# Identity products in the planned TensorE gaps of the first batch, written to a corner of a PSUM bank

## The chip, the cores and the metric

The kernel runs on one core of a Trainium2 chip. The time is the device time of one execution, in microseconds. Before the change eight executions took 437.73 to 443.24 us, with a median of 440.87 us.

## The reference

The reference is a cosine attention followed by a feed-forward layer with a quick-GELU gate:

```python
q_n = q / (np.linalg.norm(q, axis=-1, keepdims=True) + 1e-06)
k_n = k / (np.linalg.norm(k, axis=-1, keepdims=True) + 1e-06)
scores = np.matmul(q_n, k_n.transpose(0, 1, 3, 2)) / tau
attn = softmax(scores); out = np.matmul(attn, v)     # 8 batches, 12 heads, 448 tokens, 64 per head
x = out.transpose(0, 2, 1, 3).reshape(3584, 768)
h = x @ w_in                                         # 768 x 2048
y = (h * sigmoid(1.702 * h)) @ w_out                 # 2048 x 768, float32 result
```

## The kernel before

A unit y is four heads of one batch (a "duo"); a batch has three units (`ND = 3`), and there are 24. For each unit the kernel loads q, k and v, squares q and k (`sq`), adds the squares (`red`), makes inverse norms, scales q and k by them into float16 (`scale`), turns them (transposes) into the layout of the score product, multiplies (`s`), takes the exponential on ScalarE (`exp`), multiplies by v (`at`), normalises on VectorE (`nx`) and turns the result into `xT`. For the first batch the inverse norms come from ScalarE (`root`, L323: a logarithm and an exponential) and VectorE (`invert`, L328: an addition and a reciprocal for each of q and k). The feed-forward products (`mm1`, `mm2`, L618 to L682) of a batch are mixed in among the attention of later ones.

**Who sets the order.** The instructions are not issued in loop order. Every operation is registered with `plan.add` (L68) under a name such as `("tp", 1, 0)` with an engine, an estimated duration, a due time, what it must follow, and which buffer tokens it takes and frees. `Plan.order` (L102) plays this list through with the estimated durations and returns every operation with a planned start (`now`); `Plan.emit` (L85) issues them in that order. So each engine gets a fixed queue, and the program order between engines is that of the planned starts. Waits are put in afterwards, from which memory each instruction reads and writes, in program order.

**The PSUM banks.** The kernel works with eight banks of PSUM, each 512 float32 columns wide. Four are used by the two score tiles (`ps_s`, two banks each); four are single-bank tiles called `mm` (`ps_m`). Three of these rotate from the start (`mm=3` in the plan's tokens). The fourth is allocated once, at L459, for the inverse norms of the first batch: `rs_ps` is its first 84 columns. The operation `("roots", 0)` (L859), which does nothing by itself, hands it to the rotation when all six scales of the first batch are past.

**Who touches the bank of the inverse norms.** `invert` writes a reciprocal into it (L336, `mm<-n` in the profile) where the scale that will use it is planned for VectorE; for a scale on GpSimd it writes to SBUF (`rs<-n`). With the chosen engines VectorE writes the bank for `("scale", 1, 0)`, `("scale", 1, 1)` and `("scale", 0, 1)`, and those three scales read it (`qks<-qk,mm`, L404 and L405). The other three scales run on GpSimd from SBUF.

**The first operations on TensorE**, in queue order: `tp 1,0` (turn k of unit 0, seven transposes, L427), `tp 0,0`, `s 0,0,0` and `s 0,1,0` (L465), `tp 1,1`, `s 0,l,0` (L491), `tp 0,1`, `s 0,2,0`, `s 1,0,0`, `at 1,0` (L528, L539), `s 1,2,0`, `at 0,0`, and so on. ScalarE's queue at the same time: `root 1,0`, `root 0,0`, `sq 0,1`, `qkT 1,0` (copies the turned k out of PSUM, L438), `sq 0,2`, `root 1,1`, `qkT 0,0`, `sq 1,2`, `exp 0,1,0`, `qkT 1,1`, then mostly exponentials. VectorE's: `inv 1,0`, `scale 1,0`, `inv 0,0`, `red 1,1`, `red 0,1`, `inv 1,1`, `scale 1,1`, a cast of v, `scale 0,1`.

Of the kernel before, what the change touches and what calls it, by code (L numbers as in the profile page):

```python
# [10 lines left out]
FP32 = mybir.dt.float32  # L11
# [13 lines left out]
DMA_ENGINES = 16  # L25
PACKET_US = {256: 0.033, 1024: 0.072, 1536: 0.064, 1792: 0.078, 3072: 0.135, 4096: 0.178}
MOE_FROM, MOE_LAG = 8, 9
STEPS = "#$%&()*+,-./0123456789:;<=>?@ABCDEFGHIJKLMNOPQRSTUVWXYZ[]^_abcdefghijklmnopqrst"
DUES = (
    "LKQtTEKJLtIKrKKQKKK#K?MC[YRQPIKPKKK:LC3KFMKWKXgB/VK7K;eC]KKIKLWAH@@KMEKFKTTKCLKKmFBCKHQK=P>RD4S5TlMK1VkI"  # L30
# [30 lines left out]
class Plan:  # L61
# [6 lines left out]
    def add(self, name, eng, us, due, emit, after=(), takes=(), frees=(), dma=None, rows=128, hold=(), turn=False, alts=()):  # L68
        if alts:
            self.alts[name] = ((eng, us), *alts)  # L70
        after = list(after) + list(hold)
        if turn:
            self.turns.append((due, len(self.turns), name))
        self.ops[name] = (eng, us, due, emit, after, takes, frees, dma, rows, hold)

    def tune(self, dues, engines):

        engines = dict(zip(self.alts, map(int, engines)))
        for n, c in zip(list(self.ops), dues):
            eng, us, due, *more = self.ops[n]  # L80
            if n in engines:
                eng, us = self.alts[n][engines[n]]
            self.ops[n] = (eng, us, due + 0.25 * (STEPS.index(c) - 39), *more)

    def emit(self, link):  # L85


        names, done, port = list(self.ops), {}, None
        for _, i, emit in self.order():
            eng, takes, hold = self.ops[names[i]][0], self.ops[names[i]][5], self.ops[names[i]][9]  # L90
            insts = emit(eng) if names[i] in self.alts else emit()
            insts = insts or (None,) if isinstance(insts, tuple) else (insts,)
            done[names[i]] = insts[-1]
            for h in hold:
                link(insts[0], done[h])
            if ("port", 1) in takes:
                if eng == "DVE":
                    port = insts[-1]
                elif port is not None:
                    link(insts[0], port)  # L100

    def order(self):  # L102

        for n, (_, _, name) in enumerate(sorted(self.turns)):
            eng, us, due, emit, after, takes, frees, *more = self.ops[name]
            takes, frees = [*takes, (("turn", n), 1)], [*frees, (("turn", n + 1), 1)]
            self.ops[name] = (eng, us, due, emit, after, takes, frees, *more)
            self.free["turn", n + 1] = 0
# [78 lines left out]
def kernel(  # L187
# [10 lines left out]
    nc = tc.nc  # L198
# [5 lines left out]
    C = S // 64  # L204
    HP = H // 2
    ND = HP // 2
# [30 lines left out]
    ps_m = psum("ps_m", 4)  # L237
# [4 lines left out]
    ident = const.tile([128, 128], FP16)  # L242
# [213 lines left out]
        )  # L456

    tpss, sps, avps, xss = [{} for _ in range(4)]
    rs_ps = ps_m.tile([128, 512], FP32, name="mm")[:, : ND * 4 * C].rearrange("p (y t j c) -> p y t j c", y=ND, t=2, j=2)  # L459

    def score(sp, y, g, n, q0, qn, at):
        qkT = qkTs[y]
# [241 lines left out]
    def load_w_out(i):  # L704
# [5 lines left out]
    plan = Plan(  # L710
        dict(qk=NQK, v=3, sq=2, qks=4, vt=NV, qkT=NT, kL=NE, sp=2, mm=3, exp=NE)
        | {("n2", 1): 4, ("n2", 2): 2, ("nrm", 1): 4, ("nrm", 2): 8}
        | dict(xs=2, x=2 * HP, th=3, g=1, ost=2, port=1)
    )
    add = plan.add
    port = dict(takes=[("port", 1)], frees=[("port", 1)])
# [146 lines left out]
    def moe_due(b):  # L863
        return 2 * HP * (b + 1) + MOE_LAG if b else MOE_FROM
# [51 lines left out]
    total, done = sum(u[1] for u in moe), 0.0  # L916
    for name, us, emit, after, takes, frees, tail in moe:
        b, part = divmod(B * done / total, 1)
        start, end = moe_due(b), moe_due(b + 1)
# [41 lines left out]
        )  # L961

    plan.tune(DUES, ENGINES)
    plan.emit(link)
# [1 line left out]
_INS = ['q', 'k', 'v', 'tau', 'moe_w_in', 'moe_w_out']  # L966
_OUTS = [((3584, 768), 'float32')]
# [30 lines left out]
```

## Time and profile before

| What | us |
|---|---|
| median of 8 runs | 440.87 |
| lowest, highest | 437.73, 443.24 |
| the profiled execution, its own time | 440.98 |
| span of its instructions, first to last | 439.1 |
| TensorE busy in the span | 410.5 |
| VectorE, ScalarE, GpSimd busy | 289.2, 259.8, 124.9 |
| first matmul starts | 8.01 |

The span starts with the first instruction; the device time has 1.9 us more around it. TensorE is counted busy in 93% of the span; most of what is missing lies in the first 50 us. The page's clock row is 9 (full) in all slices but one: from 43 to 46 us the granted clock is 0.50. A line of a profile gives the start, the duration, the engine, the line of the kernel, what is written and read with the shapes, the number of merged instructions and, in brackets, how long the engine had been idle and who ended that.

### The profile page before, as it was taken

The page shows a single profiled execution, that of the slowest core. Times are in us where ns is not written, and L with a number is a line of the kernel's source. Part 1 is how long each engine was busy: PE and PEld are TensorE (multiplying, and loading weights), DVE is VectorE, ACT ScalarE, POOL GpSimd, SP SyncE. Part 2 cuts the span into 40 slices and gives each one's busy share as a digit, 9 for nine tenths or more (in the row PEclk, how much of TensorE's full clock was granted, in tenths as well). Part 3 has the DMA queues.
Part 4 walks back from the last instruction along what each step waited for, and adds up shares of the span by engine and source line. Part 5 has one row for each costly group of instructions (what it writes and reads, how often), then busy time and mean ns, then how long its engine had stood idle before and what let it go on. Part 6 is the DMA issues. An engine that isn't in the chain of part 4 may idle for free.

```text
span 439.1 us, 9229 instructions
## 1 busy us (share of the span) xinstructions
PE 410.5 (93%) x3614; PEld 245.9 (56%) x3614; DVE 289.2 (66%) x701; ACT 259.8 (59%) x383; POOL 124.9 (28%) x202
## 2 busy tenths in 40 slices
PE   1797999978989999999999999999999999999996
PEld 0466887543454555565555665555555556555553
DVE  6669898879997659865985958877841225414410
ACT  4878787637865568667676467667753444413300
POOL 5575251232341274432242343232320000000000
PEclk9999899999999999999999999999999999999999
DMA  8999398997768797988679978876342224020122
GB/s 273 252 218 266 76 200 201 265 218 196 163 135 212 155 211 186 176 200 186 163 165 204 172 201 171 149 151 90 56 74 64 65 65 79 1 49 24 35 74 72
DMA packets 84682, 64.88 MB, mean 148 GB/s; under 512 B 52768, under 2 KB 79648, under 8 KB 84640
## 3 DMA queue, kind: packets, MB, share of 16 engines
q1 hardware_dynamic: 80448, 57.36, 59.3%
q0 software_dynamic: 3744, 6.29, 8.0%
q8 instruction: 28, 0.46, 0.5%
q10 hardware_dynamic: 448, 0.66, 0.4%
q14 instruction: 14, 0.11, 0.1%
HBM read 47.19 MB, written 11.01 MB: 133 GB/s over the span
## 4 chain that ended last, share of the span: by engine, by line
PE 79%; DVE 9%; DMA 7%; ACT 2%; issue 2%; SPq 1%; ACTq 0%; DVEq 0%
PE mm L676 29%; PE mm L621 25%; PE mm L539 8%; PE sp L465 7%; DMA qk<-in_q_dram 6%; PE mm L651 3%; PE mm L528 3%; DVE qks L404 2%; PE sp L491 2%; DVE gT L638 2%; DVE n L313 1%; DMA qkT<-qks 1%; PE mm L427 1%; ACT exp L500 1%; DVE vt L416 1%
## 5 line engine op out<-in xcount | busy, mean ns | idle before, releaser
L500 ACT ACTIVATE exp<-sp 128x896 f16<-128x896 f32 (+1 forms) x171 | 147.0, 903 | 57.2 <-PE sp L465 50.5
L676 PE MATMUL mm<-w_out,gT 128*128 128x384 f16 x896 | 156.0, 326 | 1.4 <-DVE xs L567 1.1
L621 PE MATMUL mm<-xT,w_in 128*128 128x448 f16 x672 | 135.1, 353 | 2.2 <-DVE gT L638 1.5
L676 PEld LDWEIGHTS <-gT 128*128 128x128 f16 x896 | 84.4, 98 | 63.8 <-issue 8.9
L631 ACT ACTIVATE th<-mm 128x448 f16<-128x448 f32 x128 | 69.5, 545 | 65.1 <-PE mm L621 60.8
L621 PEld LDWEIGHTS <-w_in 128*128 128x128 f16 x672 | 63.4, 98 | 64.3 <-issue 8.3
L638 DVE SCALAR_TENSOR_TENSOR gT<-th,mm 128x448 f16<-128x448 f16 x112 | 67.8, 617 | 33.8 <-ACT th L631 30.5
L313 DVE TENSOR_REDUCE n<-sq 128x14 f32<-128x896 f32 (+1 forms) x50 | 51.7, 1043 | 13.6 <-ACT sq L305 11.7
L539 PE MATMUL mm<-vt,exp 128*128 128x65 f16 (+1 forms) x1152 | 58.2, 197 | 0.2 <-ACT exp L500 0.2
L539 PEld LDWEIGHTS <-exp 128*128 128x128 f16 (+1 forms) x1152 | 53.6, 102 | 6.2 <-issue 3.2
L465 PE MATMUL sp<-qkT 64*128 64x448 f16 (+1 forms) x324 | 42.9, 350 | 4.8 <-ACT exp L500 2.3
L528 PE MATMUL mm<-vt,exp 128*128 128x130 f16 x192 | 43.5, 227 | 3.5 <-ACT ost L690 2.4
L689 DVE TENSOR_SCALAR ost<-mm 128x384 f32<-128x384 f32 x27 | 15.0, 554 | 43.8 <-PE mm L676 43.6
L567 DVE TENSOR_TENSOR xs<-mm,rc 112x256 f16<-112x256 f32 x96 | 40.8, 425 | 3.4
L551 DVE RECIPROCAL rc<-mm 112x4 f32<-112x4 f32 x96 | 17.0, 177 | 36.5 <-PE mm L539 36.2
L305 ACT ACTIVATE sq<-qk 128x896 f32<-128x896 f32 (+1 forms) x30 | 27.3, 912 | 18.2 <-DMA qk<-in_k_dram 7.1
L416 POOL CAST vt<-v 128x384 f16<-128x384 f32 x27 | 13.7, 506 | 85.6 <-PE mm L539 31.4
L404 POOL TENSOR_TENSOR qks<-qk,y 128x384 f16<-128x384 f32 (+1 forms) x36 | 25.7, 741 | 41.6 <-DVE y L372 21.6
L690 ACT ACTIVATE ost<-mm 128x384 f32<-128x384 f32 x29 | 14.2, 489 | 31.6 <-PE mm L676 28.6
L304 POOL TENSOR_TENSOR sq<-qk 128x896 f32<-128x896 f32 (+1 forms) x14 | 23.9, 1706 | 19.6 <-DVE kL L454 6.3
L405 POOL TENSOR_TENSOR qks<-qk,y 128x896 f16<-128x896 f32 x13 | 24.2, 1865 | 18.0 <-DVE vt L421 8.4
L528 PEld LDWEIGHTS <-exp 128*128 128x128 f16 x192 | 19.3, 101 | 11.0 <-issue 7.2
(59 smaller groups left out, 261.9 us busy)
## 6 DMA issues: line engine op xcount, KB each, us to landing
v<-in_v_dram SPq DMA_DIRECT2D x48, 256.0 KB, 5.7
out_dram<-ost SPq DMA_DIRECT2D x54, 192.0 KB, 2.9
qk<-in_k_dram SPq DMA_DIRECT2D x23, 448.0 KB, 5.3
qk<-in_q_dram SPq DMA_DIRECT2D x23, 448.0 KB, 4.5
w_in<-in_moe_w_in_dram POOLq DMA_DIRECT2D x8, 384.0 KB, 13.3
w_out<-in_moe_w_out_dram POOLq DMA_DIRECT2D x2, 1536.0 KB, 13.6
qkT<-qks SPq DMA_TRANSPOSE x36, 4.5
xT<-xs SPq DMA_TRANSPOSE x18, 3.0
```

The costliest lines, as they stand in the source:

```text
L305: return nc.scalar.activation(out=dst, in_=src, func=AF.Square)
L313: return nc.vector.tensor_reduce(out=n2s[y][:, ti, js], in_=sqs[y, ti][:, js], axis=AX.X, op=ALU.add,)
L404: return tuple(eng.tensor_tensor(out=o, in0=a, in1=b, op=ALU.mult) for o, a, b in places(y))
L465: nc.tensor.matmul(out=sp[:, j, at : at + qn], lhsT=qkT[r, g, 1, 128 * n : 128 * (n + 1)], rhs=qkT[r, g, 0, q0 : q0 + qn], start=True, sto ...
L500: return nc.scalar.activation(out=dst, in_=src, func=AF.Exp, scale=inv_tau, **ekw)
L528: nc.tensor.matmul(out=o, lhsT=e[:, (C - 1) * S + a : (C - 1) * S + a + m], rhs=vt[:, 3].rearrange("p j d -> p (j d)"), start=True, stop=F ...
L539: nc.tensor.matmul(out=o[:, (D + 1) * j : (D + 1) * (j + 1)], lhsT=e[:, at : at + m], rhs=vt[:, n, j], start=False, stop=n == 2, skip_grou ...
L567: return nc.vector.tensor_tensor(out=xs, in0=ps[:, :, :D], in1=r[:, :, None].to_broadcast((P, 4, D)), op=ALU.mult,)
L621: nc.tensor.matmul(out=ps[:, :S], lhsT=w_in_sb[:, kk, 128 * m : 128 * (m + 1)], rhs=xTs[b, kk], start=(kk == 0), stop=(kk == KT1 - 1),)
L631: nc.scalar.activation(out=ths[key], in_=mms[key][:, :S], func=AF.Tanh, scale=0.851)
L638: nc.vector.scalar_tensor_tensor(out=gts[b // 2][:, m, (b % 2) * S : (b % 2 + 1) * S], in0=ths.pop((b, m)), scalar=1.0, in1=mms.pop((b, m) ...
L676: nc.tensor.matmul(out=mms[b2, t, n][:, :NW], lhsT=gts[b2][:, kk, 128 * t : 128 * (t + 1)], rhs=w_out_sb[:, kk, NW * n : NW * (n + 1)], st ...
```

## The change

`Plan.emit` gets a function `fill`. Before it issues an operation of TensorE, it looks at the planned gap between the end of TensorE's operation before and the planned start of this one, and issues identity products (128x128 by 128x128) for it. The first gap starts at a planned 2.2 us (`FILL_FROM`). Up to a planned 9.2 us a product is counted as 0.107 us, from there as 0.057 us with 0.2 us of the gap left free. It ends when `("roots", 0)` is issued. The products write columns 384 to 511 of the bank whose columns 0 to 83 are the inverse norms; nothing reads them.

```diff
+FILL_FROM, WARM_FROM, COLD_US, WARM_US = 2.2, 9.2, 0.107, 0.057
...
-    def emit(self, link):
+    def emit(self, link, fill):
-        names, done, port = list(self.ops), {}, None
-        for _, i, emit in self.order():
+        names, done, port, filled = list(self.ops), {}, None, FILL_FROM
+        for now, i, emit in self.order():
             eng, takes, hold = self.ops[names[i]][0], self.ops[names[i]][5], self.ops[names[i]][9]
+            if names[i] == ("roots", 0):
+                filled = float("inf")
+            if eng == "PE" and self.ops[names[i]][1]:
+                if now > filled:
+                    fill(filled, now)
+                filled = max(filled, now + self.ops[names[i]][1])
             insts = emit(eng) if names[i] in self.alts else emit()
...
-    rs_ps = ps_m.tile([128, 512], FP32, name="mm")[:, : ND * 4 * C].rearrange("p (y t j c) -> p y t j c", y=ND, t=2, j=2)
+    roots_ps = ps_m.tile([128, 512], FP32, name="mm")
+    rs_ps = roots_ps[:, : ND * 4 * C].rearrange("p (y t j c) -> p y t j c", y=ND, t=2, j=2)
+
+    def fill(start, end):
+        cold = max(0.0, min(end, WARM_FROM) - start)
+        warm = max(0.0, end - max(start, WARM_FROM) - 0.2)
+        for _ in range(int(cold / COLD_US) + int(warm / WARM_US)):
+            nc.tensor.matmul(out=roots_ps[:, 384:], lhsT=ident, rhs=ident, start=True, stop=True, skip_group_check=True)
...
-    plan.emit(link)
+    plan.emit(link, fill)
```

## The prediction

> **What bounds the kernel now.** I read the page first, then busy time by stretch, then the queues of single engines over the first 30 us.
>
> The page: TensorE carries the kernel, and its share is short only at the start.
>
> ```profile
> span 439.1 us, 9229 instructions
> ...
> PE 410.5 (93%) x3614; PEld 245.9 (56%) x3614; DVE 289.2 (66%) x701; ACT 259.8 (59%) x383; POOL 124.9 (28%) x202
> ...
> PE   1797999978989999999999999999999999999996
> ```
>
> Busy time by stretch, in us (TensorE, its weight loads, VectorE, ScalarE, GpSimd, each with its instructions; then granted clock, DMA share, GB/s):
>
> ```profile
> 7.00:17.00 10.00, 4.43 (x31) 2.78 (x31) 7.52 (x19) 7.02 (x12) 4.99 (x8) 1.00 1.11 277
> 17.00:30.00 13.00, 11.65 (x117) 8.03 (x118) 9.65 (x27) 10.26 (x15) 10.74 (x19) 1.00 1.12 234
> ```
>
> From 17 to 30 us TensorE is busy 11.65 of 13 us, ScalarE 10.26. Here TensorE runs at half clock, though the clock column says 1.00 (the trace has no clock record so early). Its own instructions tell it; the timeline of TensorE, seven transposes early and later:
>
> ```profile
> 10.95 0.93 PE L427 MATMUL mm<-ident,qks 128*128 128x128 f16 x7 [1.66 <-POOL qks L405]
> 14.10 0.93 PE L465 MATMUL sp<-qkT 64*128 64x224 f16 x8 [2.22 <-ACT qkT L438]
> ...
> 56.94 0.55 PE L427 MATMUL mm<-ident,qks 128*128 128x128 f16 x7
> ```
>
> One transpose lasts 0.31 us early and 0.22 us late, so the spacing is (0.93-0.31)/6 = 0.103 us slow and (0.55-0.22)/6 = 0.055 us fast. The six-product groups of L539 fall from 0.54 us (28.44) to 0.35 us (30.54): the clock rises near 29.2 us.
>
> Then VectorE and ScalarE, which hold the two queues that the change ties to TensorE:
>
> ```profile
> 7.40 1.22 DVE L404 TENSOR_TENSOR qks<-qk,mm 128x384 f16<-128x384 f32 x3
> 13.50 0.53 DVE L336 RECIPROCAL mm<-n 128x14 f32<-128x14 f32 x2
> 14.07 1.22 DVE L404 TENSOR_TENSOR qks<-qk,mm 128x384 f16<-128x384 f32 x3
> 16.08 1.09 DVE L405 TENSOR_TENSOR qks<-qk,mm 128x896 f16<-128x896 f32 x1
> ...
> 9.50 0.89 ACT L438 COPY qkT<-mm 128x896 f16<-128x896 f16 x1
> 11.94 0.95 ACT L305 ACTIVATE sq<-qk 128x896 f32<-128x896 f32 x1 [1.55 <-DMA qk<-in_q_dram]
> ```
>
> The first four are all the uses of the inverse norms' bank after the first reciprocal (7.11 us). ScalarE copies the first turned k at 9.50 and stands before a load until 11.94.
>
> **What the Trainium skill says.** "TensorE: Matmul & The Clock Gate", Part 1 (The HAM clock gate): the clock is halved by default, and a busy window of about 3.4 us, free-running, raises it; products of this shape are 107 ns apart cold, 56 ns warm. The trace agrees on the spacing (103 and 55 ns). It is less simple on the rise: TensorE was busy from 18.1 to 23.7 us and stayed slow, and at about 42.7 us the clock fell (granted 0.50 from 43 to 46 us) though it had worked 0.8 us between 40 and 42.
>
> "PSUM — Partial Sum Buffer", PSUM bank collisions raise a hardware error: two engines in the same bank and quadrant at once is an error "whether the two touch the same bytes or disjoint columns of the bank", and accesses must be guarded by bank, not by address. No run here shows it. My forecast rests on it: a corner is not a separate place, so every fill must be ordered against every VectorE access to this bank, in program order.
>
> **The change part by part.** Working the planner's list through gives the planned starts and so the fills before each TensorE operation: 66 before `tp 1,0` (planned 9.463), 30 before `tp 0,0` (11.843), 17 before `s 0,0,0` (13.463), 1 before `tp 1,1`, 6 before `s 0,l,0`, 9 before `tp 0,1`, then 13, 3, 3, 1, 18 and 8 up to the planned 24.6: 175 in all. The planned starts on VectorE are `scale 1,0` 8.323, `inv 1,1` 12.543, `scale 1,1` 13.183, `scale 0,1` 15.143. Program order follows these, so the 66 fills come *after* `scale 1,0`; the 17 after `scale 1,1`; the 6 after `scale 0,1`; and `inv 1,1` waits for the first 96, `scale 0,1` for the single one before `tp 1,1`.
>
> *The 66 fills.* They are meant for the time from 2.2 to 9.2 us, but wait for the third instruction of `scale 1,0`, 7.40+1.22 = 8.62. In TensorE's queue they stand ahead of `tp 1,0`, which began at 8.01. They start at 8.66. The clock rises one full window later, between 12.1 and 15.5 us; I take 13.8: 48 at 0.107 and 18 at 0.056 make 6.1 us, to 14.8 (limits 14.0 and 15.7).
>
> *ScalarE behind it.* `tp 1,0` takes 0.55 us, to 15.35 (was 9.29). `qkT 1,0` follows at 15.4 instead of 9.50, and blocks `sq 0,2` and `root 1,1`. In the trace each starts about 0.85 us after the one before, so the root, begun at 12.79, begins at 17.1 and ends 17.6 (was 13.26): the 2.4 us before the load are swallowed and 4.3 remain.
>
> *VectorE.* `inv 1,1` goes from 13.29 to 17.6, its reciprocals from 13.50 to 17.8. The 30 fills (15.4 to 17.1) hold nothing more. `scale 1,1` ends 19.6 (was 15.29): +4.3.
>
> *The 17 fills* wait for it: 19.65 to 20.6. So `s 0,0,0`, at 14.10 before, starts at 20.6: +6.5, and its first exponential goes from 15.07 to 21.2: +6.1. `scale 0,1`, behind the one fill, ends 22.3 (was 17.17). Six fills, then `s 0,l,0` at 22.7 (was 16.04), and the exponentials of 16.80 come at 23.1: **+6.3 us**.
>
> *What the raised clock gives back.* From there ScalarE is nearest to the path. Its waits for TensorE between 16.80 and 29.58 are, in brackets in its timeline, 0.58, 0.36, 0.51, 0.25 and 0.98 us: 2.68. With products twice as fast I expect 2.2 of them to go. The 46 remaining fills (2.6 us warm) find room: TensorE's 11.65 us shrink to some 6.5 in 13. A later start of the bank's return to the rotation costs nothing, since the plan itself counts three `mm` tokens until then. More instructions: 350, no transfers of data. **Sum: +6.3 - 2.2 = +4.1 us.**
>
> *Does it reach the end?* Later loads would absorb it if they ran by themselves. They don't: the load of unit 6 waits for the output weights, and those wait on GpSimd behind casts whose order is tied to VectorE's norms.
>
> ```profile
> 51.46 0.51 POOL L416 CAST vt<-v 128x384 f16<-128x384 f32 x1 [7.60 <-DVE y L372]
> ...
> 52.52 0.94 POOL L706 DMA_DIRECT2D w_out<-in_moe_w_out_dram  x1
> ...
> SPq L271 <- DMA w_out<-in_moe_w_out_dram: 32.6, 1, 32.6
> ```
>
> DMA carries nothing from 48 to 52 us, waiting for this. So the gate at 71.4 us moves along, and with it the chain of loads to 90 us. From 120 us on TensorE is busy 97% or more. I pass all of it on: 440.98 + 4.1 = 445.1 for the profiled run, and 0.1 less against the median of 440.87: **445.0 us**.
>
> **The rivals.**
>
> *The fills run early (faster).* If the waits went by address, the first fill would start when the identity is ready, near 1.35 us, and 66 end between 6.7 and 8.4 us; `tp 1,0` at 8.01 is hardly touched. The load at 11.94 still holds the second unit, so 8 to 17 us give little (0.5 us); from 17 to 30 us up to 2.68 us of ScalarE's waits go. That makes 440.9 - 2.5 = 438.4 us. For it speak the sizes, which fit a start at 2.2 us; against it the bank rule. It decides where the first identity product starts: 1.4 us or after 8.6.
>
> *The clock falls back (slower still).* TensorE idles from 17.6 to 19.65 us before the 17 fills, and the trace shows a fall after 2.6 us that were mostly idle. Then 17+1+6 fills, the eight score products and seven transposes run at half clock: 24 x 0.05 + 0.4 + 0.4 = 2.0 us, plus up to 0.9 from a late rise in the first block: 447 to 448. More relapses, or fills slow throughout (66 and 30 ending near 19.9, `s 0,0,0` at 23.5, over 9 us late), reach 450 and beyond.
>
> *It cancels.* A rise already at 12.1 us saves 0.8, all 2.68 us of waits go (0.5 more), and the slow phase from 43 to 46 us, which costs the kernel before about 1.7 us (half of 3.4), falls away: 4.1 - 3.0 = +1.1, 442.0 us. I find no reason for all three together; one or two leave it above 443.
>
> **How the numbers follow.** About 0.5% (2.2 us) is what a measurement of this kernel can tell from no change; single runs spread over 5.5 us. Ordered by bank with the clock raised once (443.2 to 446.5): 0.55. Falls back: 0.20. Cancels, 439 to 443: 0.15. Fills early: 0.10. Faster by over 0.5%: 0.10; within: 0.15; slower: 0.75. The range 441 to 450 leaves out the early fills and the far end of the relapses. The likeliest case alone: 443.2 to 446.5.
>
> **What would show it.** Right: identity products start near 8.66 us, released by VectorE's scale; the first transpose follows near 14 to 16 us; ScalarE stands before `qkT 1,0` about 5 us; the first exponential comes near 21 us, and everything after 35 us looks as before, some 4 us later. Wrong: identity products before 7 us; the first transpose still at 8 us; transposes still 0.103 us apart after 16 us; or the shift at 35 us not there at 72 us, where the first load after the weights would still be issued at 71.4.

## The result and the profile after

The changed kernel takes 444.48 us (median of 20 runs, 441.65 to 447.79), the kernel before 440.78 us (55 runs). The ratio is 1.0107, 95% interval 1.0088 to 1.0127: slower by 3.7 us at the medians. The profiled execution took 445.66 us with a span of 443.9 us, against 440.98 and 439.1. In this section and the next, medians are over all executions, while ratios leave out those in a slower state (more than 1.5% above the fastest of the same kernel), which matters for e6 and e10, where 7 of 22 are left out.

The page of the kernel after: 175 more TensorE instructions, 5.6 us more of TensorE busy time, the other engines as they were.

```profile
span 443.9 us, 9581 instructions
...
PE 416.1 (94%) x3789; PEld 253.5 (57%) x3789; DVE 289.0 (65%) x701; ACT 259.8 (59%) x383; POOL 125.2 (28%) x202
...
PE   2799899978989799999999999999999999999996
```

Busy time by stretch of the kernel after (columns as in the prediction). From 7 to 17 us TensorE is busy 8.03 us instead of 4.43, and ScalarE 3.58 instead of 7.02: the products run while ScalarE stands.

```profile
7.00:17.00 10.00, 8.03 (x110) 7.91 (x110) 4.52 (x11) 3.58 (x8) 4.51 (x6) 1.00 1.11 269
17.00:30.00 13.00, 10.47 (x144) 8.31 (x144) 8.48 (x22) 9.29 (x14) 7.95 (x15) 0.87 1.00 218
```

TensorE's timeline after. L472 is the identity product, L433 the transposes (L427 before), L479 the score products (L465 before). A name in brackets is who ended the idle time.

```profile
8.77 5.57 PE L472 MATMUL mm<-ident 128*128 128x128 f16 x66 [8.77 <-DVE qks L410]
14.18 0.55 PE L433 MATMUL mm<-ident,qks 128*128 128x128 f16 x7
14.57 1.84 PE L472 MATMUL mm<-ident 128*128 128x128 f16 x30
16.25 0.55 PE L433 MATMUL mm<-ident,qks 128*128 128x128 f16 x7
19.10 1.86 PE L472 MATMUL mm<-ident 128*128 128x128 f16 x17 [2.30 <-DVE qks L410]
20.89 0.93 PE L479 MATMUL sp<-qkT 64*128 64x224 f16 x8
```

The first 66 products wait for VectorE's scale (7.50 to 8.72 us, L410) and then stand in front of the first transpose, which starts at 14.18 instead of 8.01. The 17 wait for the second scale (17.83 to 19.05) and stand in front of the first score product: 20.89 instead of 14.10.

ScalarE and VectorE after:

```profile
14.77 0.91 ACT L444 COPY qkT<-mm 128x896 f16<-128x896 f16 x1 [5.07 <-PE mm L433]
15.57 0.95 ACT L311 ACTIVATE sq<-qk 128x896 f32<-128x896 f32 x1
...
17.26 0.53 DVE L342 RECIPROCAL mm<-n 128x14 f32<-128x14 f32 x2
17.83 1.22 DVE L410 TENSOR_TENSOR qks<-qk,mm 128x384 f16<-128x384 f32 x3
...
22.08 1.09 DVE L411 TENSOR_TENSOR qks<-qk,mm 128x896 f16<-128x896 f32 x1 [2.27 <-PE mm L472]
```

The copy that ran at 9.50 runs at 14.77. The square behind it no longer waits for its load; it starts 3.63 us late (15.57 against 11.94). VectorE's third scale waits 2.27 us for an identity product (L472), as the order of the bank asks.

So the shift of the chain, after minus before, is 3.76 us at the two reciprocals, 6.79 at the first exponential (21.86 against 15.07), 7.14 at the second (23.94 against 16.80), and back to 4.39 at the group of four exponentials (33.97 against 29.58). At the loads behind the output weights it is 3.70 us (75.08 against 71.38), and the span ends 4.8 us later. These are two single executions; that the 3.70 us and the 3.7 us between the medians agree so well is in part chance.

### The profile page after: what moved, and what is told of

The parts are those of the page before. It is cut to its first block, busy times and chain, and to the rows that moved or that the text cites. A ratio compares the mean times of both kernels' runs of the same rounds, so it can differ in the third digit from the quotient of the medians.

```text
span 443.9 us, 9581 instructions
## 1 busy us (share of the span) xinstructions
PE 416.1 (94%) x3789; PEld 253.5 (57%) x3789; DVE 289.0 (65%) x701; ACT 259.8 (59%) x383; POOL 125.2 (28%) x202
## 4 chain that ended last, share of the span: by engine, by line
PE 76%; DVE 8%; DMA 8%; POOL 3%; issue 2%; ACT 1%; SPq 1%; POOLq 0%; ACTq 0%; DVEq 0%
PE mm L690 28%; PE mm L635 25%; PE mm L553 7%; PE sp L479 6%; DMA qk<-in_q_dram 4%; PE mm L665 3%; DMA v<-in_v_dram 3%; PE mm L542 3%; DVE n L319 2%; PE sp L505 2%; DVE qks L410 1%; DMA qk<-in_k_dram 1%; POOL qks L411 1%; PE mm L472 1%; DVE gT L652 1%
## 5 line engine op out<-in xcount | busy, mean ns | idle before, releaser
L553 PE MATMUL mm<-vt,exp 128*128 128x65 f16 (+1 forms) x1152 | 55.8, 194 | 0.2 <-ACT exp L514 0.2
L553 PEld LDWEIGHTS <-exp 128*128 128x128 f16 (+1 forms) x1152 | 51.2, 99 | 6.3 <-issue 3.3
L542 PE MATMUL mm<-vt,exp 128*128 128x130 f16 x192 | 42.6, 222 | 4.2 <-ACT ost L704 2.5
L479 PE MATMUL sp<-qkT 64*128 64x448 f16 (+1 forms) x324 | 41.4, 336 | 2.1 <-ACT exp L514 2.1
L410 POOL TENSOR_TENSOR qks<-qk,y 128x384 f16<-128x384 f32 (+1 forms) x36 | 25.8, 743 | 41.7 <-DVE y L378 21.7
```

The costliest lines, as they stand in the source:

```text
L410: return tuple(eng.tensor_tensor(out=o, in0=a, in1=b, op=ALU.mult) for o, a, b in places(y))
L479: nc.tensor.matmul(out=sp[:, j, at : at + qn], lhsT=qkT[r, g, 1, 128 * n : 128 * (n + 1)], rhs=qkT[r, g, 0, q0 : q0 + qn], start=True, sto ...
L542: nc.tensor.matmul(out=o, lhsT=e[:, (C - 1) * S + a : (C - 1) * S + a + m], rhs=vt[:, 3].rearrange("p j d -> p (j d)"), start=True, stop=F ...
L553: nc.tensor.matmul(out=o[:, (D + 1) * j : (D + 1) * (j + 1)], lhsT=e[:, at : at + m], rhs=vt[:, n, j], start=False, stop=n == 2, skip_grou ...
```

## The experiments

Each ratio is against the kernel before on the same chip, with its 95% interval.

| run | what is issued | ratio | interval |
|---|---|---|---|
| the change | 175 products, shared bank | 1.0107 | 1.0088 to 1.0127 |
| e1 | only the first 66, shared bank | 1.0147 | 1.0112 to 1.0183 |
| e2 | only the other 109, shared bank | 1.0053 | 1.0024 to 1.0082 |
| e3 | one product in each place, shared bank | 1.0056 | 1.0026 to 1.0086 |
| e7 | 20 before the first transpose, shared bank | 1.0061 | 1.0037 to 1.0085 |
| e11 | 55, after VectorE's last use of the bank | 1.0028 | 1.0005 to 1.0051 |
| e6 | 60 ahead of everything, shared bank | 1.0001 | 0.9973 to 1.0030 |
| e4 | 175, inverse norms in SBUF | 1.0004 | 0.9985 to 1.0024 |
| e5 | none, inverse norms in SBUF | 1.0026 | 1.0004 to 1.0047 |
| e8 | 175, each block in a bank of its own | 0.9991 | 0.9967 to 1.0016 |
| e9 | 157, own banks, 12 before `tp 0,0` | 0.9970 | 0.9947 to 0.9993 |
| e10 | 79, own banks, from `s 0,0,0` on | 0.9988 | 0.9964 to 1.0012 |
| e12 | 20 before the first transpose, own bank | 1.0038 | 1.0013 to 1.0064 |

### Is it the shared bank? (e8)

The same 175 products in the same places of the queue; only the bank that they write is another one. (Each block takes the next tile of the rotation, so the tiles after it land in other banks than before.)

```diff
-        for _ in range(int(cold / COLD_US) + int(warm / WARM_US)):
-            nc.tensor.matmul(out=roots_ps[:, 384:], lhsT=ident, rhs=ident, ...)
+        n = int(cold / COLD_US) + int(warm / WARM_US)
+        own = n and ps_m.tile([128, 512], FP32, name="mm")
+        for _ in range(n):
+            nc.tensor.matmul(out=own[:, 384:], lhsT=ident, rhs=ident, ...)
```

> All 175 products in the same places of the queue as in the changed kernel, but each block writes into a tile of its own from the rotating mm banks; the inverse norms stay alone in their bank. The only thing changed is which bank is shared. Theory (the shared bank is the whole loss): first product near 1.4 us and the first 66 end near 7.5, first transpose near 8.0, first score product at 14.1 to 15, the second scale and its copy no later than before; the clock is up before 17 us, and the loads behind the output weights are issued 1.5 to 3 us earlier than at 71.4: 438.5 us, 437 to 440. Rival (products in these places cost time whatever bank they write): 443 us or more. Third (a gain at 72 us is lost again afterwards, as the run with the norms in SBUF suggests with 69.5 there and 440.5 at the end): 440 us.

The loss is gone: 0.9991, 439.77 us against 440.56. TensorE's timeline of this run:

```profile
1.38 6.50 PE L474 MATMUL mm<-ident 128*128 128x128 f16 x66 [1.38 <-POOL ident masks.py:199]
9.81 0.23 PE L433 MATMUL mm<-ident,qks 128*128 128x128 f16 x1 [1.93 <-DVE qks L410]
10.28 0.77 PE L433 MATMUL mm<-ident,qks 128*128 128x128 f16 x6 [0.24 <-DVE qks L410]
10.84 3.25 PE L474 MATMUL mm<-ident 128*128 128x128 f16 x30
```

The first 66 now start when the identity is ready, 7.4 us earlier than in the changed kernel, and nobody waits for them. The 30 behind the first transpose are not free: at half clock they take 3.25 us, the second transpose starts at 13.92 instead of 10.95, and ScalarE stands before its copy:

```profile
14.52 0.91 ACT L444 COPY qkT<-mm 128x896 f16<-128x896 f16 x1 [1.29 <-PE mm L433]
```

That the same products cost 1.07% in one bank and nothing measurable in another settles the main question: it is the order that the shared bank imposes, not the work. One thing stays open: a tile of `ps_m` fills a whole bank, so no run here tells whether the waits go by bank or by tile.

The expected 438.5 us did not come. In this profile the head is ahead by 3.5 us at 71 us (the load is issued at 67.85), but the span ends only 2.0 us earlier, and the median of all runs is only 0.8 us lower. The profile shows where most of this lead goes. The pair of exponentials that starts at 84.89 us in the kernel before starts at 81.34, 3.55 us ahead; the next one starts at 97.72 against 99.73, only 2.01 ahead. Between them the clock is halved, after TensorE had done 0.16 us of work from 86 to 88 us (columns as above, the granted clock behind GpSimd's count):

```profile
86.00:88.00 2.00, 0.16 (x5) 0.16 (x5) 1.16 (x2) 1.33 (x2) 0.00 (x0) 1.00 1.99 341
88.00:90.00 2.00, 2.00 (x21) 1.17 (x19) 1.90 (x7) 0.00 (x0) 1.26 (x4) 0.72 1.09 71
90.00:92.00 2.00, 2.00 (x22) 1.61 (x21) 0.65 (x3) 0.87 (x1) 1.33 (x1) 0.50 0.74 169
```

The profiles of e9 and e10 have the same fall and lose 1.5 and 1.3 us between the same exponentials; those of e12 and e11, ahead by 2.0 and 1.4 us without this fall, lose none. Why TensorE stands at 86 us (I take it, for the loads of the next units) is not shown, nor how often the fall comes in executions without a profile.

### The norms moved away instead (e4, e5)

The products stay in the bank and the norms go to SBUF; e5 is the control without products.

```diff
-            if plan.ops["scale", ti, y][0] == "DVE":
-                rss[y, ti] = rs_ps[:, y]
-            else:
-                rss[y, ti] = p_n.tile([128, 2, 2, C], FP32, name="rs", bufs=4)
+            if (y, "t") not in rss:
+                rss[y, "t"] = p_n.tile([128, 2, 2, C], FP32, name="rs", bufs=3)
+            rss[y, ti] = rss[y, "t"]
```

> All 175 products, but the inverse norms are kept in SBUF, so the bank holds nothing but the products and nothing on VectorE has to be ordered against them. Theory: the first product starts when the identity is ready, near 1.4 us; 66 end between 6.7 and 8.4 us; the first transpose stays near 8.0 us, no later block waits for VectorE, and TensorE is warm from 5 to 8 us on: 438.4 us, 437 to 440.5. Rival (the products themselves cost the time, by standing in TensorE's queue): no faster than the changed kernel, 443 us or more. Third (a raised clock is worth nothing here since ScalarE is the bound): 440.8 us, with the transposes fast and the exponentials where they were.

> The kernel before with the inverse norms of the first batch in SBUF instead of PSUM, and no products. The control for the run with products and SBUF. Both theories: 440.8 us, within 1 us; the three scales on VectorE that read the norms may change by 0.1 us each.

Again the loss is gone (1.0004) and the third outcome holds rather than 438.4 us. The control alone reads 1.0026: in its profile the first scale took 2.71 us on VectorE (7.54 to 10.25) instead of 1.22. That is not the price of SBUF as such, since in e4 the same scale from SBUF took 1.23 us; in e5 a square on GpSimd ran beside it from 7.69 to 9.63. Between e4 and its control lie 0.0022, and the intervals overlap.

### Which block costs what (e1, e2)

```diff
-                if now > filled:
+                if now > filled and names[i] == ("tp", 1, 0):   # e1; e2 has != instead
```

> Only the 66 products before the first transpose are left; the other 109 are not issued. Theory (products wait for the bank's readers, then hold up the queue): the first product starts near 8.7 us, the first transpose near 14.2, ScalarE's second root ends near 16.9 as in the changed kernel, so VectorE's second scale is again 3.7 us late; but the first score product follows its copy near 17.8 us instead of waiting for 17 products until 20.9. The clock is warm for a while, so some of it is given back: 442.5 us, 441.5 to 444.5. Rival (the loss is the sum of TensorE time spent on identity products, whatever they wait for): 66 of 175 products are some 7.4 of 15 us cold, so about half of the 3.7 us: 442.6 us as well, but with the score product at 20.9 minus 3.7. The times of the first score product and of the second scale decide, and this run together with the next.

> The 66 products before the first transpose are left out, the other 109 are issued as in the changed kernel. Theory: the first transpose is back at 8.0 us and the second scale ends near 15.3 us as before; the 17 products still wait for it and, with the clock not yet raised, take 1.8 us, so the first score product moves from 14.1 to about 17.2 us (+3.1) and the scale of q of unit 1 from 16.1 to about 18.2 us; with the clock raised afterwards about 2 us come back: 442.3 us, 441 to 444. Rival (the first block is the whole loss): as before, 440.8 us, or faster by the raised clock.

e1 is the larger surprise: the first block alone reads 1.0147, no better than the whole change (from six executions; the intervals touch). Its start is as expected, and its first score product comes at 17.75 us, as foreseen. But then the clock is lost. TensorE's timeline of e1, and below it the busy time of the stretch 20 to 30 us, where the granted clock (the number after GpSimd's count) is 0.50:

```profile
14.19 0.94 PE L433 MATMUL mm<-ident,qks 128*128 128x128 f16 x14
17.75 0.56 PE L479 MATMUL sp<-qkT 64*128 64x224 f16 x8 [2.62 <-ACT qkT L444]
...
21.00 0.93 PE L433 MATMUL mm<-ident,qks 128*128 128x128 f16 x7 [1.16 <-DVE qks L411]
```

```profile
20.00:22.00 2.00, 1.00 (x9) 0.79 (x11) 1.98 (x3) 1.62 (x3) 1.86 (x3) 0.50 0.24 50
...
28.00:30.00 2.00, 1.79 (x15) 1.08 (x16) 1.33 (x3) 1.78 (x3) 2.00 (x3) 0.50 1.12 210
```

Without later products the clock stays halved from about 19.6 to 33.2 us, and none of the delay comes back: 3.86 us late at 33.44 (29.58 before) and 4.2 at the loads. So the first block alone makes the whole loss. In the change the later ones first add to it (7.14 us at the second exponential, where e1 has 3.47) and then, with the clock up, give 2.75 back; at 34 us the change is still 0.5 us later than e1. That the later products help is therefore not shown.

e2 has the other half. The first transpose is back at 7.96 us; the 17 products wait for the second scale (15.29) and move the first score product to 16.33, +2.2 us where I had +3.1, because the clock had risen near 13 us. By 29.93 us only 0.35 of it is left, and its profile ends earlier than that of the kernel before (span 438.0), though its median is 0.53% above.

### The wait without the work (e3), and a small first block (e7, e12)

e3 issues at most one product in each place. e7 issues 20 before `tp 1,0` and none elsewhere, e12 the same 20 in a bank of their own.

```diff
-        for _ in range(int(cold / COLD_US) + int(warm / WARM_US)):
+        for _ in range(min(1, int(cold / COLD_US) + int(warm / WARM_US))):     # e3
...
+                if now > filled and names[i] == ("tp", 1, 0):                  # e7, e12
+                    fill(7.0, 9.2)
```

> One product in each place where the changed kernel has a block, in the same bank: the waits without the work, 12 products instead of 175. Theory: the wait alone moves the first transpose from 8.0 to 8.8 us, the first score product from 14.1 to about 15.4, the scale of q of unit 1 by 0.5 to 1 us; nothing raises the clock early: 441.4 us, 440.5 to 442.5. Rival (the waits by themselves are the loss): 443 us or more.

> 20 products before the first transpose, none elsewhere. Theory: they take 2.1 us from 8.7 to 10.9, the first transpose starts near 10.8 instead of 8.0, but ScalarE stands before a load until 11.9 anyway, so its copy near 11.6 delays that square and everything behind it by only 0.5 us: 441.0 us, 440 to 442. Rival (every microsecond that the first transpose is late is lost): 2.8 us late, 443 us.

> The 20 products before the first transpose, which cost 0.6% in the shared bank, in a tile of their own. Theory: they run from 1.4 to 3.5 us beside the loads and change nothing: 440.6 us, 439.8 to 441.5. Rival (the 0.6% came from products being there at all, or from the loads being shifted by chance): 442 to 443.5 us.

e3 measures 1.0056, about 2.5 us where I had 0.8. In its profile one product waits for the second scale, in front of the first score product:

```profile
15.61 0.27 PE L472 MATMUL mm<-ident 128*128 128x128 f16 x1 [3.43 <-DVE qks L410]
15.81 0.93 PE L479 MATMUL sp<-qkT 64*128 64x224 f16 x8
```

It moves the first score product to 15.81 (+1.7), and the next pair of waits makes it +2.0 at the second exponential (18.81 against 16.80) and +2.1 at 31.72. Nothing gives it back, since the clock rises no earlier. A dozen products of 0.1 us are enough for this delay: what they wait for is the price.

e7 was a miss: 1.0061 where I expected next to nothing. Its profile shows the expected part, the first transpose at 10.57 us and its copy at 11.56, but the square behind the load began at 13.21 and not at 12.4, for the load landed later than in the kernel before: ScalarE stood 0.74 us before it, so in this profile the 20 products themselves delayed nothing here. When this load lands differs between executions: the square starts at 11.94 us in the kernel before, at 11.50 in e11 and at 11.31 in e12. e12 was a miss as well: 20 products that nobody waits for read 1.0038, while its profiled execution, with its first score product at 13.48, was ahead of the kernel before. e7 minus e12 is 0.0023, or 1.0 us, where the expectation had 0.5, but the intervals overlap, and the two ran on different chips. What the remaining 0.4% of e12 is, stays open. With e5 and e11 it says that kernels which should be alike here differ by 0.3 to 0.4%, so I read no mechanism from differences of that size.

### Early products, and products after the last reader (e6, e11)

e6 issues 60 products ahead of the plan, in the shared bank, so that VectorE's first reciprocal comes behind them; e11 issues only those planned after VectorE's last use of the bank.

```diff
-                if now > filled:
-                    fill(filled, now)
...
+    fill(2.2, 8.7)                                  # e6, ahead of plan.emit
...
+                if now > filled and now > 16:       # e11
+                    fill(filled, now)
```

> 60 products issued ahead of everything else in program order, so that VectorE's first reciprocal waits for them and not they for VectorE; none later. Theory: they run from 1.4 to about 7 to 7.8 us; the first reciprocal is 0 to 0.6 us late; TensorE then stands nearly idle between its transposes until 14 us, so the clock falls back and nothing is gained: 440.6 us, 439.8 to 441.8. Rival (a warm start by itself is worth something): 439 us or less.

> The shared bank as in the changed kernel, but only the 55 products whose place comes after VectorE's last use of the inverse norms (from the one before the fourth transpose on). Theory: nothing waits for anything that it did not wait for before; the fourth transpose starts near 17.2 to 17.9 us, the clock rises between 20 and 26 instead of 29 us: 439.8 us, 438.8 to 441.2. Rival (sharing a bank costs time by itself, without a wait): 442 us or more.

e6 is the same bank and nearly the first block of the change, with the program order turned round:

```profile
1.38 5.67 PE L470 MATMUL mm<-ident 128*128 128x128 f16 x60 [1.38 <-POOL ident masks.py:199]
...
14.42 0.93 PE L477 MATMUL sp<-qkT 64*128 64x224 f16 x8 [2.35 <-ACT qkT L442]
```

The products ran from 1.38 to 7.05 us; the first transpose started at 7.99, warm (six in 0.51 us), and by 14.42 the score products were slow again (0.93 us). The ratio is 1.0001, while the median over all executions, 442.17 us, lies 1.6 us above the 440.56 of the kernel before and outside the expected range. Either is far from e1, which issues 66 such products behind the reciprocal and reads 1.0147. So the order decides, and nothing shows that a warm start that is not kept is worth anything.

e11 started its later products without any new wait (the first nine wait for the same scale as the transposes behind them, which they hold up by 0.9 us) and had the clock up by 20.5 us (four score products in 0.37 us). In its profile it was 0.92 us ahead at 28.66, while the ratio reads 1.0028, within the differences that I don't read.

### A version to beat both (e9, e10)

```diff
+                    fill(filled + 1.0 * (names[i] == ("tp", 0, 0)), now)      # e9, own banks
...
+                if now > filled and now > 12:                                 # e10, own banks
```

> Products in tiles of their own from the rotating banks, as before, but 12 instead of 30 before the second transpose, where the clock had fallen back and 30 took 3.2 us. Theory: the second transpose starts 1.5 to 2 us earlier than with 30 (near 12 instead of 13.9 us), its copy no longer waits, and the first score product comes near 14.2; the loads behind the output weights are issued near 68 us: 439 us, 437.5 to 440.2. Rival (whatever is gained at the head is lost to the loads between 72 and 90 us): as with 30, 440 us.

> Products in tiles of their own, and only the 79 from the one before the first score product on; no early ones. Theory: the first score product is hardly moved from 14.1 us (17 products cold are 1.8 us and end near 13.8), the clock rises near 17 to 20 us instead of 29, and about 2 us of ScalarE's waits go: 438.8 us, 437.5 to 440.2. Rival (cold products in short gaps cost as much as the clock gives back): 440.6 us or more.

e9 is the only one whose interval lies below the kernel before, 0.9970 (439.00 against 439.96 us). Its first score product came at 14.06 us, as foreseen, but in its profiled execution (443.50 us) the loads were issued at 72.12 and not near 68. e10 reads 0.9988, and its median over all executions, 441.23 us, is 1.3 us above the kernel before. The gain of e9 is as small as the differences that I leave unread, so I don't claim it. Against the changed kernel, by way of the kernel before, the ratios of e8, e9 and e10 are all lower by about 1%.

## Why the prediction was right

**The bound (right).** The head is a chain from TensorE through ScalarE's copy to VectorE, and a shift there reaches the end: 3.7 us at 75 us, 4.8 at the end of the profile, 3.7 between the medians. One reading in it was off: from 120 to 200 us TensorE of the kernel before is busy 77.11 of 80 us (96%) and from 400 us on 34.74 of 39, not 97% or more; nothing followed from it.

**The waits by bank (right; this decided it).** The 66 products started at 8.77 us (8.66 foreseen), released by VectorE's scale. e8 moved the start to 1.38 by changing the bank, and e6 by changing the order. The Trainium skill's page "PSUM — Partial Sum Buffer", in its section on bank collisions, asks for guards by bank and not by address; the trace agrees in so far as products on columns 384 and up waited for accesses to columns 0 to 83 (8.77 us, the scale ending at 8.72). Whether the waits go by bank or by tile, and whether a collision would be an error, was not tried.

**The first block (right, 0.5 us too long).** The clock rose near 12.4 us, inside the limits of 12.1 and 15.5 but well before the 13.8 that I took. The block ended near 14.3 instead of 14.8, so `inv 1,1` was 3.64 us late and not 4.3, and the second scale 3.76.

**The 17 products and the single ones (right in kind, undersized).** I had 0.95 us for the 17 and +6.3 us at the second exponential; they took 1.86 and it was +7.14. The cause is the event of my slower rival: the clock fell back at about 19.3 us, after TensorE had been idle from 16.80 to 19.10, and was halved until 22.7. So the rival's mechanism and the likeliest case's time came together, because the first block was shorter and more was given back than I had assumed. I had treated these as exclusive, and they were not. That the sum still came within 0.5 us of the measured median is in part luck: a term left out and terms too small on the other side made up for each other.

**What the raised clock gives back (right, 0.5 us too small).** 7.14 fell to 4.39 at the group of four exponentials: 2.75 us where I took 2.2. Up to the loads another 0.7 us came back, where the halved clock from 42.7 to 46 us of the kernel before did not occur: from 44 to 50 us the granted clock was 1.00. I had put that into the rival in which all cancels. It need not be the work of the products: the profile of e5, which issues none, has no halved clock there either, and that of e9, with products and a clock raised early, has one.

**The faster rival (wrong about its size).** Where the fills do run early, e8 and e4 read 439.8 and 440.5 us, not 438.4. My estimate counted ScalarE's waits up to 30 us and passed them to the end. In e8 the lead did reach 71 us (3.5 us), but 1.5 us of it went with a further fall of the clock near 89 us; e4 led by 1.9 us at the loads and its span ends only 0.5 us earlier, for reasons that stay open. The changed kernel's delay did pass: it stood at 3.70 us at the loads and at 4.8 us at the end.

## What to carry to other kernels

In this kernel an unused corner of a bank was not free as long as another engine worked in that bank: its accesses were ordered against each other, and work that was meant to fill a gap waited for the end of the gap and took its time after it. Before placing filler work, look up in the program order what stands ahead of it and who waits behind it, and give it a bank that nobody else touches. A clock raised early and lost again before the dense work brought nothing that was measured here (e6), and one raised by 7 us and kept up to 27 us (the profile of e9) came with no more than 0.3%.

## What the runs showed of the hardware

The clock falls sooner than I assumed. The Trainium skill's page "TensorE: Matmul & The Clock Gate", Part 1, speaks of an idle window of about 3.4 us. In the changed kernel the last matmul before the gap ended at 16.80 us, the clock fell at about 19.3 and rose at about 22.7: 2.5 us of rest sufficed, and the halved phase lasted 3.4 us. In e8 it fell near 10.4 us, again 2.5 us after the products ended at 7.88, with one or two transposes in between. In e6 it fell near 12.75, after 0.57 us of work in the 3.4 us before. The changed kernel in stretches of 3.41 us:

```profile
12.44:15.85 3.41, 3.41 (x64) 3.41 (x62) 0.00 (x0) 1.08 (x2) 0.11 (x1) 1.00 1.14 227
15.85:19.26 3.41, 1.11 (x21) 0.99 (x18) 2.16 (x7) 2.71 (x5) 1.39 (x5) 1.00 1.09 241
19.26:22.68 3.42, 3.42 (x33) 2.73 (x31) 1.14 (x4) 0.82 (x1) 2.55 (x4) 0.50 0.73 213
```

The rise at 12.44, the fall at 19.26 and the rise at 22.68 lie whole multiples of 3.41 us apart, and so do 29.14, 42.80 and 46.21 in the kernel before. A fall came at the end of such a stretch though TensorE had been busy 1.11 us of it (here) or 1.65 us (39.38 to 42.80 in the kernel before): the rest need not fill it. Nor is a busy stretch always enough for a rise: from 18.90 to 22.31 us TensorE of the kernel before was counted busy throughout, and the clock stayed halved until about 29.14.

A small operation on VectorE can take as long as a large one beside it on GpSimd. In e8 an addition over 128x14 took 1.66 us; in the changed kernel it took 0.16. The two lines of e8, VectorE and GpSimd:

```profile
7.23 1.66 DVE L336 TENSOR_SCALAR n<-n 128x14 f32<-128x14 f32 x1
...
7.17 1.68 POOL L310 TENSOR_TENSOR sq<-qk 128x896 f32<-128x896 f32 x1 [1.57 <-DMA qk<-in_k_dram]
```

They end together at 8.85 to 8.89 us. In the changed kernel the addition ran at 7.02, before the square's start at 7.64. In e8 and e4, where the two met (1.66 and 1.31 us for the addition), the first transpose started at 9.81 and 9.64 us, against 8.01 in the kernel before: a shift of 1.6 to 1.8 us, more than most of what was compared here. That the one held up the other is argued from these times; no run here separates them.
